# Batch 0 of an attention and mixer kernel: the first weights are decoded earlier, the last tile's products with v stand ahead of the turning, and the two blocks alternate from chunk 0

## The chip, the core and the metric

The kernel runs on one core of a Trainium2 chip. The metric is the device time of one execution in microseconds (us), and the time of a kernel is the median of its runs. TensorE (PE in the profile) multiplies, VectorE (DVE) and ScalarE (ACT) work on vectors, GpSimd (POOL) does a few copies, and SyncE (SP) issues the transfers between memory and the chip's buffers (DMA). Each engine takes its instructions strictly in the order in which they were written into its queue; semaphores hold an instruction back until its data or its buffer is there.

## What is computed

The reference, cut to what matters (four batches of 768 tokens, 8 heads of 64; the mixer's weights are 64-bit floats):

```python
# attention: chunks of 32 queries; each sees 16 keys to the left, its own 32, 8 to the right, and 8 memory slots
scores = scale * np.matmul(q_c, k_full.transpose(0, 1, 3, 2))
a = softmax(scores)                      # row maximum taken off, sum + 1e-9
out[:, :, c_start:c_end] = np.matmul(a, v_full)
# mixer, on x = attention's output, (4, 768, 512)
h = x.transpose(0, 2, 1) @ U @ V         # U 768x32, V 32x768
u = x + h.transpose(0, 2, 1)
ch = np.maximum(u @ w_ch1, 0.0) @ w_ch2  # 512 -> 2048 -> 512
return u + ch
```

## The kernel before

**Tiles and blocks.** A batch's 768 tokens are six tiles of 128 for the mixer (`xs[(b, t)]`), and two blocks of three tiles. Attention works in three tiles T of 256 tokens: `k_part` and `q_part` turn k and q, `s_turn` multiplies them, `s_weights` and `s_sums` make the softmax, `t_part` turns the weights, and `av_part(T)` (line 618) multiplies them with v and lets VectorE scale the product into two tiles x (line 629). `collect(t)` (line 641) sums x times U over all six tiles in one bank; the sum `g` is split into a high and a low part (lines 894 and 895).

**The mixer's input, transposed.** The mixer needs u transposed, a chunk c of 128 channels at a time, four chunks. For batch 0, `turn_x` (line 934) turns block 0 of x by multiplying it with the identity, and leaves the banks open; `join_uT` (line 943) adds V times g to the same banks, and ScalarE and VectorE split each sum into `uh` and `ul` (lines 947 and 948). `turn_x1` and `join_uT1` (lines 958, 975, 979 and 980) do the same for block 1, a chunk at a time.

**Weights.** w1 and w2 come as 64-bit floats in 16 chunks f of 128 hidden channels. The generator `stream` decodes them. A decode is: ScalarE takes the high word of each number (`begin`, line 202); VectorE shifts (209), masks (217), multiplies the low word in (222) and adds (229); ScalarE casts the sum to the high part (340); VectorE subtracts to get the low part (344). The pieces of chunks 0 and 1 (w1 and w2 of each apart) have 512 numbers a row, later ones 1024. `advance(n)` runs `stream` up to its n-th next `yield`: where `advance` stands in the program is where the decode's instructions stand in the queues of ScalarE and VectorE.

**The feed-forward part.** A step of a block with a chunk f is `w1_step` (line 1205: 12 products, high by high, low by high, high by low, into one bank; then ScalarE makes `hh`, line 1213, and VectorE `hl`, line 1214) and, one step later, `w2_step` (lines 1256 and 1262: 9 products into three accumulators). `both_blocks` runs the steps of batch 0. Its list `units` takes block 0 and block 1 in turn for chunks 0 to 10 (`SPLIT` is 11), block 1 `LEAD` chunks behind block 0, and then chunks 11 to 15 of one block after the other. Block 1's accumulators are the three banks of `ps_a` up to unit 21; VectorE adds them to x in unit 22 (line 1221), and the turning of batch 1's keys (line 486), which starts in unit 23, takes the same banks.

**What sets the order.** TensorE's and SyncE's queues stand as the program is written. VectorE's does up to unit 22 and ScalarE's up to unit 2; from there a scheduler orders them by priorities, and the steps' `hh` and `hl` have a high one. `keep_clock(n)` puts n products of a tile of zeros ahead of the next bank's use (line 131).

Of the kernel before, what the change touches and what calls it, by code (L numbers as in the profile page):

```python
# [30 lines left out]
CHAIN = [2, 4]  # L31
WLO = 4
HIGH = 400
LEAD = 1
SPLIT = 11
EARLY = 5
NDEC = 3
# [17 lines left out]
def chunk_attn_then_mixer_kernel(  # L55
# [79 lines left out]
    def keep_clock(n):  # L135

        warm[0] += n
# [213 lines left out]
    def stream():  # L351

        work = [[(f, n)] for f in range(NSOLO) for n in range(2)] + [[(f, 0), (f, 1)] for f in range(NSOLO, NF)]

        def ready(n):
            return n < len(work) and work[n][0][0] in staged and not (front[0] and len(work[n]) > 1)

        def begun(n):
            words = Words([raw for f, which in work[n] for raw in staged[f][which]], nc.vector)
            words.begin()  # L360
            return words

        while not ready(0):
            yield
        ahead, before = begun(0), []
        yield
        for n, parts in enumerate(work):
            while ahead is None and not ready(n):
                yield
            words, ahead = ahead or begun(n), None  # L370
            words.shift()
            if before:
                if len(parts) > 1:
                    yield
                for part in before:
                    lower(*part)
            if ready(n + 1):
                ahead = begun(n + 1)
            yield
            words.power()  # L380
            if len(parts) > 1:
                yield
            words.mantissa()
            yield
            val = words.join()
            before = [(f, which, val[:, 512 * m:512 * m + 512]) for m, (f, which) in enumerate(parts)]
            before = [part + upper(*part) for part in before]
            yield
        for part in before:
            lower(*part)  # L390
        yield
# [13 lines left out]
    def attention(b, xs):  # L405
# [246 lines left out]
        if b == 0:  # L652
# [89 lines left out]
            for t in two:  # L742
                collect(t)
            yield
            av_part(1)
            spread_v(val)
            advance(1)
            for t in two:
                collect(2 + t)
            wide[0] = None  # L750
            early = turn_x()
            advance(3)
            yield
            keep_clock(GAP[3])
            av_part(2)
            advance(1)
            keep_clock(CHAIN[0])
            for t in range(4, NT):
                collect(t)
            turned.extend(turn_x1(c) for c in range(2))  # L760
            yield
        else:
            mv = sm.tile([P, 4 * D], F32, name="mv")
# [133 lines left out]
            )  # L897
        if b == 0:
            join_uT(early, g3)
            for c in range(2):  # L900
                join_uT1(turned[c], c, g3)
            rest.extend((c, g3) for c in range(2, NCK))
        yield "joined"
        if b > 1:
            yield
# [19 lines left out]
    uT = {}  # L925
    w1ls = {}

    def turn_x():

        banks = [ps_h.tile([P, 512], F32, name="ps_h") for _ in range(2)]  # L930
        banks += [ps_o.tile([P, 512], F32, name=f"acc{i}") for i in range(2)]
        for c in range(NCK):
            for tt in range(TB):
                nc.tensor.matmul(
                    out=banks[c][:, tt * P:(tt + 1) * P], lhsT=xs[(0, tt)][:, c * P:(c + 1) * P],
                    rhs=ident, start=(tt == 0), stop=False, skip_group_check=True,
                )
        return banks
# [257 lines left out]

    def w1_step(b, blk, f, w1l, between=lambda: None):
        uh, ul = uT[(b, blk)]
        ph = att_ps() if f == 0 and (b, blk) == (0, 0) else ps_h.tile([P, 512], F32, name="ps_h")
        parts = [(w1h[f], uh, c) for c in range(NCK)] + [(w1l, uh, c) for c in range(NCK)]  # L1200
        parts += [(w1h[f], ul, c) for c in range(NCK)]
        if f > 1 or (b, blk) != (0, 0):
            parts = [part for c in range(NCK) for part in (parts[c], parts[8 + c])] + parts[4:8]
        for m, (w, u, c) in enumerate(parts):
            nc.tensor.matmul(  # L1205
                out=ph[:, :TOK], lhsT=w[:, c, :], rhs=u[c], start=(m == 0), stop=(m + 1 == len(parts)),
            )
            if m + 1 == len(parts) // 2:
                between()
        hh = hid.tile([P, TOK], F32R, name="hh")  # L1210
        hl = hid.tile([P, TOK], F32R, name="hl")
        with tc.high_priority(offset=HIGH):
            nc.scalar.activation(out=hh, in_=ph[:, :TOK], func=AF.Relu)  # L1213
            nc.vector.scalar_tensor_tensor(  # L1214
                out=hl, in0=ph[:, :TOK], scalar=0.0, in1=hh.bitcast(F32), op0=ALU.max, op1=ALU.subtract,
            )
        return hh, hl
# [53 lines left out]
    def both_blocks(following):  # L1271
# [12 lines left out]
        for n, (blk, f, where, begins, ends) in enumerate(units):  # L1284
# [20 lines left out]
                    next(gen[0])  # L1305
                    taken[0] += 1

            hid_ = w1_step(0, blk, f, w1l, between)
            if n == 1:
                for c, g3 in rest:  # L1310
                    join_uT1(turn_x1(c), c, g3)
            for _ in range(RATE + (n % 4 > 0)):
                advance(1)
                more_w()
# [134 lines left out]
```

## Time and profile before

| | us |
|---|---|
| median of 3 runs | 683.27 (681.65 to 685.68) |
| the profiled execution's own time | 685.91 |
| its span, first to last instruction | 683.8 |
| TensorE busy | 648.7 |
| VectorE busy | 345.2 |
| ScalarE busy | 234.7 |
| DMA, mean over the span | 156 GB/s |

The span is what the instructions fill; the execution's own time has 2.1 us around it. A busy TensorE may still run at half its clock: the profile gives the granted clock beside the busy time. A wait is listed as "engine, what it writes, its line <- engine, what it wrote, its line", with the total, the number and the longest.

### The profile page before, as it was taken

Reading aid. Unit: us, or ns where it says so; the run is one execution under the profiler, and the core shown is the slowest. Engines: PE = TensorE matmul, PEld = TensorE weight load, DVE = VectorE, ACT = ScalarE, POOL = GpSimd, SP = SyncE. Lnnn points to the kernel's source line nnn. Section 1 sums busy time; section 2 is a strip of 40 time slices with the busy share of each in tenths; the row PEclk is TensorE's granted clock in tenths of the full one; section 3 lists DMA queues with packets and bytes.
Section 4 is the critical chain, followed back from the end, with each engine's and each line's share of the span. In section 5 each row is a group of like instructions: output and inputs, shape, how many; then the busy total and the mean of one; then the engine's idle time right before and its main releaser. Section 6 shows DMA issues by size and latency. Waiting matters only on the chain.

```text
span 683.8 us, 15135 instructions
## 1 busy us (share of the span) xinstructions
PE 648.7 (95%) x6184; PEld 563.7 (82%) x6188; DVE 345.2 (50%) x681; ACT 234.7 (34%) x574; POOL 63.0 (9%) x95
## 2 busy tenths in 40 slices
PE   7776999998999899999999998999999999999997
PEld 4555999997877599898888887999978889999886
DVE  5847777799554443426424562434436732222322
ACT  4524434434622125323122433434223611212221
POOL 2000000021100042233343000000000000000000
PEclk9998999999999999999999999999999999999999
DMA  8887265434571296762955449884733035555301
GB/s 234 156 254 273 94 210 168 154 118 135 132 149 49 84 271 183 217 205 86 288 191 157 139 129 253 203 207 130 195 104 108 1 108 166 172 144 180 123 2 46
DMA packets 121548, 106.37 MB, mean 156 GB/s; under 512 B 51240, under 2 KB 91048, under 8 KB 121480
## 3 DMA queue, kind: packets, MB, share of 16 engines
q1 hardware_dynamic: 121480, 105.41, 53.1%
q8 instruction: 49, 0.80, 0.5%
q14 instruction: 19, 0.16, 0.1%
HBM read 79.30 MB, written 25.17 MB: 153 GB/s over the span
## 4 chain that ended last, share of the span: by engine, by line
PE 86%; DVE 5%; SPq 3%; DMA 2%; issue 2%; ACT 1%; ACTq 0%; DVEq 0%
PE acc L1256 22%; PE ps_h L1205 19%; PE ps_h L1134 18%; PE acc L1262 11%; PE ps_a L618 2%; PE ps_a L486 2%; PE ps_a L545 2%; PE ps_a L1256 2%; PE ps_a L599 1%; PE acc L641 1%; PE acc L1250 1%; PE ps_a L908 1%; DMA w1l<-w1s 1%; PE ps_a L647 1%; PE ps_a L1262 1%
## 5 line engine op out<-in xcount | busy, mean ns | idle before, releaser
L1256 PE MATMUL acc<-w,hh 128*128 128x512 f32 x606 | 159.5, 398 | 0.0
L1256 PEld LDWEIGHTS acc<-w,hh 128*128 128x128 f32 x606 | 111.1, 189 | 21.3 <-issue 1.0
L1205 PE MATMUL ps_h<-uh,w1h 128*128 128x384 f32 x252 | 87.4, 349 | 7.3 <-ACT w1h L340 6.6
L1262 PE MATMUL acc<-w,hl 128*128 128x512 f32 x303 | 87.6, 397 | 0.0
L1205 PE MATMUL ps_h<-ul,w1h 128*128 128x384 f32 x252 | 85.8, 343 | 1.8 <-DVE ul L997 1.8
L1214 DVE SCALAR_TENSOR_TENSOR hl<-ps_h,hh 128x384 fp32r<-128x384 f32 x63 | 35.0, 555 | 88.5 <-ACT hh L1213 88.4
L1213 ACT ACTIVATE hh<-ps_h 128x384 fp32r<-128x384 f32 x63 | 30.8, 489 | 125.3 <-PE ps_h L1205 125.3
L1262 PEld LDWEIGHTS acc<-w,hl 128*128 128x128 f32 x303 | 55.5, 188 | 11.8 <-issue 0.8
L1205 PEld LDWEIGHTS ps_h<-uh,w1h 128*128 128x128 f32 x252 | 48.3, 192 | 10.5 <-ACT w1h L340 6.9
L1205 PE MATMUL ps_h<-uh,w1l 128*128 128x384 f32 x252 | 56.4, 347 | 0.0
L1205 PEld LDWEIGHTS ps_h<-ul,w1h 128*128 128x128 f32 x252 | 48.5, 192 | 4.4 <-DVE ul L997 2.1
L1205 PEld LDWEIGHTS ps_h<-uh,w1l 128*128 128x128 f32 x252 | 46.4, 193 | 0.0
L1134 PE MATMUL ps_h<-t34h,w1l 128*128 128x384 f32 x128 | 39.4, 349 | 0.0
L1134 PE MATMUL ps_h<-bh,w1l 128*128 128x384 f32 x128 | 36.7, 346 | 2.5 <-DMA w1l<-w1s 2.5
L1134 PE MATMUL ps_h<-t12h,w1l 128*128 128x384 f32 x128 | 37.4, 347 | 0.0
L1151 DVE TENSOR_TENSOR c<-ps_h,c 128x384 f32<-128x384 f32 x16 | 8.9, 558 | 55.3 <-PE ps_h L1134 54.6
L1144 DVE SCALAR_TENSOR_TENSOR hl<-hst,hh 128x384 fp32r<-128x384 f32 x32 | 17.8, 556 | 27.8 <-PE acc L1262 27.7
L1151 DVE TENSOR_TENSOR hst<-ps_h,hst 128x384 f32<-128x384 f32 x32 | 17.8, 555 | 24.2 <-ACT hst L1155 24.2
L1143 ACT ACTIVATE hh<-hst 128x384 fp32r<-128x384 f32 x32 | 16.8, 525 | 36.8 <-PE acc L1256 32.4
L1020 POOL TENSOR_TENSOR vb<-w1h,w1l 128x512 f32<-128x512 f32 x16 | 20.6, 1294 | 92.0 <-DMA w1l<-w1ld 92.0
L910 DVE TENSOR_TENSOR x<-ps_a,x 128x512 f32<-128x512 f32 x24 | 16.4, 689 | 23.1 <-PE ps_a L908 23.1
L1134 PEld LDWEIGHTS ps_h<-bh,w1l 128*128 128x128 f32 x128 | 24.0, 192 | 3.4 <-issue 2.8
(233 smaller groups left out, 1088.5 us busy)
## 6 DMA issues: line engine op xcount, KB each, us to landing
w1l<-w1s SPq DMA_DIRECT2D x112, 256.0 KB
w1l<-w1ld SPq DMA_DIRECT2D x35, 256.0 KB
w1s<-sums SPq DMA_DIRECT2D x32, 256.0 KB
rw<-in_moe_w_ch_dram SPq DMA_DIRECT2D x14, 512.0 KB
qraw<-in_q_dram SPq DMA_DIRECT2D x24, 256.0 KB
out_dram<-x SPq DMA_DIRECT2D x24, 256.0 KB
vb<-in_v_dram SPq DMA_DIRECT2D x56, 98.0 KB
raw<-in_moe_w_ch_dram SPq DMA_DIRECT2D x20, 256.0 KB
```

The source lines that it names most:

```text
L486: nc.tensor.transpose(out=psv[:, p, r, :], in_=half[:, r, 2 * p:2 * p + 2, :].rearrange("n h d -> n (h d)"), identity=ident,)
L910: nc.vector.tensor_tensor(out=x, in0=hp, in1=x, op=ALU.add)
L1020: nc.gpsimd.tensor_tensor(out=v2 if odd else v1, in0=hi, in1=lo, op=ALU.add)
L1134: nc.tensor.matmul(out=ps[:, :TOK], lhsT=w_, rhs=u, start=(start and m == 0), stop=(m == 5), skip_group_check=True,)
L1143: nc.scalar.activation(out=hh, in_=c, func=AF.Relu)
L1144: nc.vector.scalar_tensor_tensor(out=hl, in0=c, scalar=0.0, in1=hh.bitcast(F32), op0=ALU.max, op1=ALU.subtract,)
L1151: nc.vector.tensor_tensor(out=out, in0=ps[:, :TOK], in1=in1, op=ALU.add)
L1205: nc.tensor.matmul(out=ph[:, :TOK], lhsT=w[:, c, :], rhs=u[c], start=(m == 0), stop=(m + 1 == len(parts)),)
L1213: nc.scalar.activation(out=hh, in_=ph[:, :TOK], func=AF.Relu)
L1214: nc.vector.scalar_tensor_tensor(out=hl, in0=ph[:, :TOK], scalar=0.0, in1=hh.bitcast(F32), op0=ALU.max, op1=ALU.subtract,)
L1256: nc.tensor.matmul(out=acc[tt], lhsT=h[:, sl], rhs=w, start=(begins and m == 0), stop=False,)
L1262: nc.tensor.matmul(out=acc[tt], lhsT=hl[:, sl], rhs=w2h[f], start=False, stop=ends is not None)
```

## The change

Line numbers of the kernel before are used for both kernels in the text; in the changed kernel the same statements stand 2 to 6 lines further down.

- **Decode.** `advance(5)` now stands ahead of `av_part(1)`, `advance(3)` behind the sums of tiles 2 and 3, `advance(2)` behind `av_part(2)`, and another ahead of the joins. `stream` yields at the same points for short and long pieces, and begins a short piece's successor after `mantissa` and not after `shift`.
- **Order on TensorE.** `turn_x` is split by chunks: `av_part(2)` stands ahead of all of it, chunks 0 and 1 are turned behind `av_part(2)`, then come the sums of tiles 4 and 5, then chunks 2 and 3.
- **Block 1's chunks.** Three of block 1's four chunks (two before) are turned and joined ahead of the first step; the fourth is turned inside the first step, between its sixth and seventh product (before, chunks 2 and 3 behind the second step).
- **The units.** `LEAD` is 0: the first steps are (block 0, chunk 0), (block 1, chunk 0), (0, 1), (1, 1) and so on, where they were (0, 0), (0, 1), (1, 0), (0, 2), (1, 1). The first step takes the bank `acc2`, and not one of `ps_a`.

```diff
-LEAD = 1
+LEAD = 0
...
             if before:
-                if len(parts) > 1:
-                    yield
+                yield
                 for part in before:
                     lower(*part)
-            if ready(n + 1):
+            if len(parts) > 1 and ready(n + 1):
                 ahead = begun(n + 1)
             yield
             words.power()
-            if len(parts) > 1:
-                yield
+            yield
             words.mantissa()
             yield
+            if ahead is None and ready(n + 1):
+                ahead = begun(n + 1)
...
             yield
+            advance(5)
             av_part(1)
             spread_v(val)
-            advance(1)
             for t in two:
                 collect(2 + t)
+            advance(3)
             wide[0] = None
-            early = turn_x()
-            advance(3)
             yield
             keep_clock(GAP[3])
             av_part(2)
-            advance(1)
-            keep_clock(CHAIN[0])
+            advance(2)
+            early = turn_x(two)
             for t in range(4, NT):
                 collect(t)
-            turned.extend(turn_x1(c) for c in range(2))
+            early += turn_x(range(2, NCK))
+            keep_clock(CHAIN[0])
+            turned.extend(turn_x1(c) for c in range(3))
+            advance(2)
             yield
...
             join_uT(early, g3)
-            for c in range(2):
+            for c in range(3):
                 join_uT1(turned[c], c, g3)
-            rest.extend((c, g3) for c in range(2, NCK))
+            rest.extend((c, g3) for c in range(3, NCK))
...
-    def turn_x():
+    def turn_x(cs):
-        banks = [ps_h.tile([P, 512], F32, name="ps_h") for _ in range(2)]
-        banks += [ps_o.tile([P, 512], F32, name=f"acc{i}") for i in range(2)]
-        for c in range(NCK):
+        banks = []
+        for c in cs:
+            ps = ps_h.tile([P, 512], F32, name="ps_h") if c < 2 else ps_o.tile([P, 512], F32, name=f"acc{c - 2}")
+            banks.append(ps)
             for tt in range(TB):
                 nc.tensor.matmul(
-                    out=banks[c][:, tt * P:(tt + 1) * P], lhsT=xs[(0, tt)][:, c * P:(c + 1) * P],
+                    out=ps[:, tt * P:(tt + 1) * P], lhsT=xs[(0, tt)][:, c * P:(c + 1) * P],
...
-        ph = att_ps() if f == 0 and (b, blk) == (0, 0) else ps_h.tile([P, 512], F32, name="ps_h")
+        first_step = f == 0 and (b, blk) == (0, 0)
+        ph = ps_o.tile([P, 512], F32, name="acc2") if first_step else ps_h.tile([P, 512], F32, name="ps_h")
...
-            hid_ = w1_step(0, blk, f, w1l, between)
-            if n == 1:
+            def joins():
                 for c, g3 in rest:
                     join_uT1(turn_x1(c), c, g3)
+                advance(2)
+
+            hid_ = w1_step(0, blk, f, w1l, between if n else joins)
```

What this makes of the queues is shown at two places. First, VectorE around attention's tiles 1 and 2 of batch 0; `x<-ps_a,rs` is the scaling behind `av_part` (line 629), `dec` the buffer of a decode, `rw_213` and `raw` the raw words of w1's chunk 0, and line 581 ends the softmax sums of tile 2. One piece of the difference:

```order
 L580 TENSOR_SCALAR rs<-rs 128x16
 L581 RECIPROCAL rs<-rs 128x16
+L209 TENSOR_SCALAR dec<-dec 128x512
+L217 TENSOR_SCALAR dec<-dec 128x512
+L222 SCALAR_TENSOR_TENSOR dec<-rw_213,dec 128x256
+L222 SCALAR_TENSOR_TENSOR dec<-raw,dec 128x256
+L229 TENSOR_TENSOR dec<-dec 128x512
 L629 TENSOR_TENSOR x<-ps_a,rs 128x256
 L629 TENSOR_TENSOR x<-ps_h,rs 128x256
```

Five instructions, the decode of w1's chunk 0, moved from behind tile 1's x to ahead of it. Further down in VectorE's queue, before (`rw_217` is w2's chunk 0, `g_983` the sum with U, `ul` block 0's low part, `ul_1003` block 1's):

```order
L229 TENSOR_TENSOR dec<-dec 128x512
L629 TENSOR_TENSOR x<-ps_a,rs 128x256 x4
L209 TENSOR_SCALAR dec<-dec 128x512
L344 TENSOR_TENSOR w1l<-dec,w1h_889 128x512
L895 TENSOR_TENSOR g_983<-acc_341,g_983 32x256 x2
L948 TENSOR_TENSOR ul<-ps_h,uh 128x384 x2
L948 TENSOR_TENSOR ul<-acc_868,uh 128x384
L948 TENSOR_TENSOR ul<-acc_869,uh 128x384
L980 TENSOR_TENSOR ul_1003<-ps_a,uh_1002 128x384 x2
L217 TENSOR_SCALAR dec<-dec 128x512
L222 SCALAR_TENSOR_TENSOR dec<-rw_217,dec 128x512
L229 TENSOR_TENSOR dec<-dec 128x512
```

and in the changed kernel (the last row is the low part of w2's chunk 0):

```order
L209 TENSOR_SCALAR dec<-dec 128x512
L344 TENSOR_TENSOR w1l<-dec,w1h_787 128x512
L217 TENSOR_SCALAR dec<-dec 128x512
L629 TENSOR_TENSOR x<-ps_a,rs 128x256 x4
L222 SCALAR_TENSOR_TENSOR dec<-rw_217,dec 128x512
L229 TENSOR_TENSOR dec<-dec 128x512
L209 TENSOR_SCALAR dec<-dec 128x512
L344 TENSOR_TENSOR w_958<-dec,w_958 128x512
```

The decode of w2's chunk 0 stood behind the six splits of `uh` and `ul`; now it ends ahead of the sum `g`.

Second, VectorE at the end of the alternating units, where block 1's accumulators are added to x (`x<-ps_a,x`, three of them). `hl` is unit 22's, `vb_108` and `vb_109` hold decodes of 1024 numbers a row. Before:

```order
L229 TENSOR_TENSOR vb_108<-vb_108 128x1024
L1214 SCALAR_TENSOR_TENSOR hl<-ps_h,hh 128x384
L229 TENSOR_TENSOR vb_109<-vb_109 128x1024
L1221 TENSOR_TENSOR x<-ps_a,x 128x512 x3
L344 TENSOR_TENSOR w1l<-vb_108,w1h_1913 128x512
```

and in the changed kernel:

```order
L222 SCALAR_TENSOR_TENSOR vb_108<-rw_1617,vb_108 128x512
L209 TENSOR_SCALAR vb_109<-vb_109 128x1024
L1218 SCALAR_TENSOR_TENSOR hl<-ps_h,hh 128x384
L1225 TENSOR_TENSOR x<-ps_a,x 128x512 x3
L229 TENSOR_TENSOR vb_108<-vb_108 128x1024
```

Both joins (line 229) that stood ahead of the three additions stand behind them now.

## The prediction

> **What bounds the kernel now.** The page gives TensorE 648.7 of 683.8 us, so time is won only where it waits or runs slowly. I read first the list of TensorE's waits.
>
> ```profile
> PE ps_h L1205 <- ACT w1h L340: 6.6, 1, 6.6
> PE ps_a L486 <- DVE x L1221: 3.0, 1, 3.0
> PE ps_h L618 <- issue: 2.8, 1, 2.8
> ```
>
> The longest is the second step's wait for the high part of w1's chunk 1. Second, the chain of waits around it (start, length, what):
>
> ```profile
> 42.90 1.89 PE ps_h L934 x12
> 44.78 1.34 PE acc L934 x12
> ...
> 46.55 1.48 PE ps_a L618 x91
> 48.03 0.75 DVE x L629 x2
> ...
> 48.82 1.96 PE acc L641 x4
> ...
> 51.05 1.50 PE ps_a L958 x12
> 52.55 0.19 PE ps_h L943
> ...
> 53.34 1.88 DVE ul L948 x4
> ...
> 62.21 0.63 ACT w1h L340
> ...
> 62.88 4.21 PE ps_h L1205 x12
> ...
> 69.19 1.38 PE acc L1256 x6
> 70.57 0.69 PE acc L1262 x3
> 71.25 2.10 PE ps_h L1205 x12
> ```
>
> TensorE stops at 56.3 (62.88 less the wait of 6.6) and then needs 4.21 us for twelve products that take 2.10 at 71.25. Third, the stretches of 3.41 us by granted clock (columns: stretch, its length, busy time of PE, PEld, DVE, ACT, POOL, clock, DMA share, GB/s):
>
> ```profile
> 37.10:40.51 3.41, 1.63 (x18) 0.69 (x18) 1.47 (x5) 0.92 (x4) 0.00 (x0) 1.00 0.72 153
> 40.51:43.92 3.41, 3.41 (x9) 2.04 (x9) 3.28 (x8) 1.20 (x3) 0.00 (x0) 0.50 0.64 183
> 54.16:57.58 3.42, 2.12 (x10) 1.60 (x10) 3.35 (x8) 0.99 (x3) 0.00 (x0) 1.00 1.06 400
> 57.58:60.99 3.41, 0.00 (x0) 0.00 (x0) 2.71 (x7) 1.57 (x3) 0.00 (x0) 1.00 0.78 297
> 60.99:67.82 6.83, 4.94 (x17) 4.95 (x18) 5.28 (x11) 4.08 (x9) 0.00 (x0) 0.50 0.46 145
> 163.39:166.80 3.41, 3.41 (x13) 3.02 (x13) 3.41 (x7) 2.50 (x10) 0.00 (x0) 0.50 0.39 122
> ```
>
> A stretch with 1.63 us of work is followed by one at half clock, one with 2.12 is not. So the wait costs twice: 6.6 us, and half of the 4.94 us of work at half clock behind it, 2.47. The second wait of the list,
>
> ```profile
> 162.57 0.30 PE L486 MATMUL ps_a<-ident,kn 128*128 128x128 f32 x1 [3.04 <-DVE x L1221]
> ```
>
> costs 3.04 plus half of the 3.41 at half clock behind it: 4.75.
>
> Why is chunk 1 late? VectorE's timeline (the bracket is the idle time before):
>
> ```profile
> 39.01 0.42 DVE L629 TENSOR_TENSOR x<-ps_a,rs 128x256 f32<-128x256 f32 x1 [3.91 <-PE ps_h L618]
> ...
> 41.57 0.43 DVE L209 TENSOR_SCALAR dec<-dec 128x512 int32<-128x512 int32 x1
> ...
> 43.29 0.69 DVE L229 TENSOR_TENSOR dec<-dec 128x512 f32<-128x512 f32 x1
> 48.01 1.42 DVE L629 TENSOR_TENSOR x<-ps_a,rs 128x256 f32<-128x256 f32 x4 [4.03 <-PE ps_a L618]
> ```
>
> It idles 3.91 us and 4.03 us behind the softmax sums and behind its first decode, each time for a tile's products with v, and decodes the rest when the joins are over.
>
> **The change, part by part.** I follow TensorE from 42.90, up to which its queue is the same, to the end of the first step's `w2_step`. Before, that is at 71.25, with two `w1_step`s and all eight joins done; in the changed kernel the same work is done at the same mark, so the difference of the two times is the gain.
>
> *Decode ahead of tile 1's x.* Five instructions now stand ahead of 39.01. They took 2.41 us (41.57 to 43.98). VectorE is free from 35.10 (39.01 less 3.91), ScalarE's copies take 0.43 more, and the words must have landed:
>
> ```profile
> 30.14 0.46 SPq L300 DMA_DIRECT2D raw<-in_moe_w_ch_dram  x1
> ```
> ```profile
> 31.10:36.00 4.90, 4.75 (x126) 2.57 (x125) 3.83 (x11) 0.59 (x1) 0.00 (x0) 0.74 1.11 257
> ```
> ```profile
> 40.72 0.43 ACT L202 ACTIVATE dec<-raw 128x256 f32<-128x256 f32 x1
> ```
>
> The two halves are issued by 30.60 and are read, without a wait, from 40.72. Between 31.10 and 36.00 the DMA moved 4.90 x 257 KB = 1.26 MB, more than chunk 0's 1 MB. I take 36.0 as the landing: 36.0 + 0.43 + 2.41 = 38.84, just ahead of 39.01, cost nothing. The bounds: nothing, and, landing only at 40.72, 40.72 + 0.43 + 2.41 - 39.01 = 4.55 us, since x and all behind it queue behind the decode.
>
> *Products with v ahead of the turning.* From 42.90: two warming products at half clock 0.85 (they took 46.12 to 46.55 at full), products with v 1.48: 45.23. VectorE makes tile 4's x in 0.75 (row 48.03), hidden behind six turnings of 1.34: 46.57. The sums 1.96: 48.53; six more turnings 1.34: 49.87; warming 0.27 (50.78 to 51.05): 50.14; nine turnings of block 1 at 1.50 for six, 2.25: 52.39. Meanwhile `g` is split: before, that took at most from 50.78 to the first join at 52.55, 1.77; now 48.53 + 1.77 = 50.30, plus up to 0.69 behind the low part of w2's chunk 0, which stands ahead of it on VectorE: hidden with 1.4 to spare. The wait of 0.79 for x (48.03 to 48.82) and the one for `g` are gone.
>
> *Joins and first step.* Seven joins of 0.19 from 52.39: 53.72. The first four products need all four `uh`; the fourth `uh` was there before the fourth `ul` began, three quarters of 1.88 after 53.34, so at most 2.2 after the first join: 54.6; three products of 0.175 (2.10 / 12): 55.1. Now the fourth chunk's turning needs a bank that VectorE frees: `ul` of block 0 ran from 0.79 after the first join (53.34 against 52.55) for 1.88, then one more of 0.5: 52.39 + 0.79 + 1.88 + 0.5 = 55.56. TensorE waits 0.4 to 0.7, a new wait inside the step; behind it on TensorE stand six products of the step, and ScalarE's `hh` waits for those. The stretch keeps more than 2.12 us of work, so the clock stays. Turning 0.67 (half of 1.34) and join 0.19: 56.4; six products: 57.5; the second step's twelve 2.10: 59.6; `w2_step` 1.38 + 0.69: **61.6**. The gain at the mark is 71.25 - 61.6 = 9.65 us.
>
> *Chunk 1 in the changed kernel.* VectorE ends block 1's last `ul` some 1.2 after its join at 56.4 (0.79 + 0.5 as above): 57.6. Mask and two low words at 0.43 (41.57 to 43.29 is four such), `hl` 0.55, join 0.69: 60.1; ScalarE's cast 0.63: 60.8, ahead of 61.6. A second `hl` waits for its `hh`, which stands behind the cast: 61.3 + 0.55 + the low part's 0.69 = 62.5, due after four products, at 62.3: a wait of 0.2. Then w2's chunk 1 (0.43 + 0.69 + 0.69), a shift (0.68), a low part (0.69) and `hl` (0.55): 66.2; chunk 2's mask, low words and join (0.68 + 1.7 + 1.21) and its cast: 70.4, due at 61.8 + 2 x 4.15 = 70.1: a wait of 0.3. I take 0.5 for both; the bounds are 0 and 1.5 (VectorE's 12 us a tenth slower).
>
> After that the decode gains on TensorE:
>
> ```profile
> 79.60:120.00 40.40, 40.40 (x206) 37.01 (x205) 31.29 (x51) 17.16 (x37) 0.00 (x0) 1.00 0.53 175
> ```
>
> VectorE works 31.29 of 40.40 us here, 6.43 of the 8.30 us of a pair of steps (2 x 4.15). With `LEAD` 0 a chunk is due one step later than before in the list, and the rate is the same. The number of products, transfers and decodes doesn't change; In SyncE's queue one store of w1's low part (line 322), which waits for VectorE, now stands ahead of chunk 3's loads; chunk 3 is due in the seventh step, and the store's data is made before tile 2's x.
>
> *Unit 22.* In VectorE's queue two joins of 1024 numbers leave the place ahead of the additions that free `ps_a`:
>
> ```profile
> 153.07 0.55 DVE L1214 SCALAR_TENSOR_TENSOR hl<-ps_h,hh 128x384 fp32r<-128x384 f32 x1
> ```
> ```profile
> 160.14 0.54 DVE L1214 SCALAR_TENSOR_TENSOR hl<-ps_h,hh 128x384 fp32r<-128x384 f32 x1
> 160.61 1.21 DVE L229 TENSOR_TENSOR vb<-vb 128x1024 f32<-128x1024 f32 x1
> 161.74 0.68 DVE L1221 TENSOR_TENSOR x<-ps_a,x 128x512 f32<-128x512 f32 x1
> ```
> ```profile
> L222 DVE SCALAR_TENSOR_TENSOR vb<-rw,vb 128x512 f32<-128x512 uint32 (+1 forms) x11 | 6.2, 565 | 0.1
> ...
> L344 DVE TENSOR_TENSOR w1l<-vb,w1h 128x512 fp32r<-128x512 f32 x5 | 3.4, 686 | 0.2
> L217 DVE TENSOR_SCALAR vb<-vb 128x1024 int32<-128x1024 int32 x5 | 3.4, 685 | 0.0
> ```
>
> From unit 21's `hl` to the first addition it took 8.67 us. Now there stand between them one join (1.21), three shifts and masks (0.685 each), two low parts (0.686 each), a chunk's low words (three, at most 1.7) and two `hl` (0.55 each): 7.4 us at the means of 79.6 to 120 (last fence), and 8.7 if the list without `hl` runs a fifth slower beside GpSimd's copies. The wait of 3.04 shrinks by 1.3 or not at all; I take 1.0, so 2.0 is left, and half a chance of the half clock (0.85): 2.85 in place of 4.75, a gain of 1.9. Bounds: 0, and 3.0 (1.7 left, clock kept).
>
> [...]
>
> [...]
>
> **The sum.** -9.65 + 0.5 - 1.9 = -11.05. The profiled execution of 685.91 (span 683.8) would become 674.9. It lies 2.64 above the median of the runs, so against the median: 683.27 - 11.05 = **672.2**.
>
> **The rivals.**
> *Late words.* w1's chunk 0 lands near 40.7; VectorE, strictly in order, holds tile 1's x behind the decode. For: 1.11 as DMA share, the queues are full. Against: the bytes. Price 4.55: 676.7.
> *The decode stays the bound.* Chunks 1 to 3 each come late, since VectorE has done less of its list at the mark. Waits 1.5 instead of 0.5, and unit 22 gains nothing: 683.27 - 8.15 = 675.1.
> *Given back.* Batch 1's keys are loaded by the list of pieces, and GpSimd waited for them:
>
> ```profile
> 148.20 1.58 POOL L435 COPY kn<-kraw 128x512 f32<-128x512 f32 x2 [121.92 <-DMA kraw<-in_k_dram]
> ```
>
> If their landing doesn't come earlier with TensorE, unit 23 waits out the gain of the front: some 682.5. Against: these copies end 12.8 us before the turning that needs them (162.57), and SyncE issues the loads where the pieces stand.
> *Slower.* In the alternating units VectorE needs more than 8.30 us a pair, from 1.29 times its 6.43 on. If its low parts ran as the next row has them, 1.09 against 0.69, a pair would take 10.2, and ten pairs 19 us more: 683.27 - 9.2 + 19 = 693.
>
> ```profile
> 150.24 1.09 DVE L344 TENSOR_TENSOR w1l<-vb,w1h 128x512 fp32r<-128x512 f32 x1
> ```
>
> Against: those long ones came beside GpSimd's copies, and GpSimd did nothing for 121.92 us before 148.20.
>
> **How the numbers follow.** Forecast 0.72, late words 0.10, decode bound 0.09, given back or nothing done 0.05, slower 0.04. A measurement of this kernel tells 0.5%, 3.4 us, from no change. Faster by more: the first three, 0.91, less 0.02 for a mishap with code loading (the 2.8 us wait that names no releaser, which may come again at a new place): 0.89. Within: 0.06. Slower: 0.05. The range: the most that can come off is 9.65 + 3.0 = 12.65, 670.6, and half the spread of the runs shown (681.65 to 685.68) is 2.0: 668.6; late words, 676.7, with the same 2.0 make the upper end, 678.7.
>
> **What would show it.** Right: no wait of 6.6 for `w1h`; VectorE's two idle stretches filled or gone; `w2_step` of the first step ending near 61.6; no half clock between 44 and 150; a wait of less than 3 at line 486. Wrong: x of tile 1 later than 39.0, waits for `w1h` or `w1l` in many units, or TensorE waiting for keys in unit 23.

## The result, and the profile after

| | before | changed |
|---|---|---|
| median of 15 runs, us | 681.85 | 676.03 |
| ratio, 95% interval | | 0.9909 (0.9886 to 0.9931) |
| the profiled execution's own time, us | 685.91 | 673.55 |
| its span, us | 683.8 | 671.6 |
| TensorE busy, us | 648.7 | 642.6 |

The change is faster by 6.2 us (681.85 x 0.0091; by the interval 4.7 to 7.8). The forecast was 11.05. One run of the changed kernel, 1712.74 us, was disturbed and is left out of the ratio.

The list of TensorE's waits, changed kernel (line numbers are now those of its own text: as before up to line 641, 2 to 6 higher from line 889 on; "issue" means that the trace shows nothing that ended the wait):

```profile
PE ps_a L618 <- issue: 2.9, 3, 1.1
...
PE ps_a L486 <- DVE pt L568: 1.9, 1, 1.9
PE ps_h L618 <- issue: 1.9, 1, 1.9
...
PE ps_a L486 <- DVE x L1225: 1.5, 1, 1.5
```

The 6.6 for `w1h` is gone, and the 3.0 in front of batch 1's keys is now 1.5. New is a wait of 1.9 at the same line 486, for `pt`, a softmax of batch 1. The chain of waits from the second group of sums with U to the end of the first step's `w2_step` (start, length, what):

```profile
41.46 2.08 PE acc L641 x3
43.54 0.22 PE ps_a L131
43.90 1.28 PE ps_a L618 x77
45.19 0.79 issue
45.98 0.42 PE ps_a L618 x23
46.40 1.53 PE ps_h L937 x12
47.93 1.72 PE acc L641 x4
49.65 1.34 PE acc L937 x12
...
51.26 2.17 PE ps_a L961 x18
53.43 0.19 PE ps_h L946
...
60.94 1.36 PE acc L1260 x6
62.30 0.69 PE acc L1266 x3
62.99 1.08 PE ps_h L1209 x6
```

The sums end at 43.54 and the mark, the end of the first `w2_step`, is at 62.99, so 19.45 us; before it was 42.90 to 71.25, 28.35. Inside the moved products with v TensorE stands for 0.79, and the trace names nothing that ended this wait.

VectorE and ScalarE at the moved decode (timelines; the bracket is the idle time before):

```profile
36.62 0.46 ACT L202 ACTIVATE dec<-raw 128x256 f32<-128x256 f32 x1 [0.32 <-DMA raw<-in_moe_w_ch_dram]
```
```profile
37.11 0.43 DVE L209 TENSOR_SCALAR dec<-dec 128x512 int32<-128x512 int32 x1 [1.30 <-ACT dec L202]
...
38.83 0.69 DVE L229 TENSOR_TENSOR dec<-dec 128x512 f32<-128x512 f32 x1
39.44 0.42 DVE L629 TENSOR_TENSOR x<-ps_a,rs 128x256 f32<-128x256 f32 x1
```

The words of chunk 0 were waited for until 36.62; tile 1's x then follows the decode with no idle time, at 39.44. It lost nothing by that here: the last of tile 1's products with v ended at 39.39.

The new wait, on TensorE and then on VectorE:

```profile
173.55 0.63 PE L486 MATMUL ps_a<-ident,kn 128*128 128x128 f32 x4 [1.93 <-DVE pt L568]
```
```profile
170.76 0.55 DVE L1218 SCALAR_TENSOR_TENSOR hl<-ps_h,hh 128x384 fp32r<-128x384 f32 x1
171.38 0.18 DVE L555 MEMSET ps_a<- 32x64 f32 x2
171.52 1.29 DVE L567 TENSOR_REDUCE mx<-ps_a 128x8 f32<-128x512 f32 x2
172.73 1.27 DVE L568 TENSOR_TENSOR pt<-ps_a,mx 128x512 f32<-128x512 f32 x2
```

A turning of batch 1's keys needs a bank of `ps_a`, and the two banks of scores are read by VectorE until 174.0. In the kernel before, VectorE had time to spare at the same place, 2.75 us ahead of the addition that comes before this `hl`:

```profile
178.99 0.69 DVE L910 TENSOR_TENSOR x<-ps_a,x 128x512 f32<-128x512 f32 x1 [2.75 <-PE ps_a L908]
```

In the changed kernel the same addition (line 912, 169.18) has no idle time before it. This `hl` starts 9 us earlier than before (170.76 against 179.60), the last low part of the decode ends only 5 earlier (170.84 against 176.24).

### The profile page after: what moved, and what is told of

It reads as the page before. It is cut to its first block, busy times and chain, and to the rows that moved or that the text cites. A ratio compares the mean times of both kernels' runs of the same rounds, so it can differ in the third digit from the quotient of the medians.

```text
span 671.6 us, 15133 instructions
## 1 busy us (share of the span) xinstructions
PE 642.6 (96%) x6184; PEld 557.3 (83%) x6188; DVE 343.9 (51%) x681; ACT 234.2 (35%) x574; POOL 64.1 (10%) x95
## 2 busy tenths in 40 slices
DMA packets 121548, 106.37 MB, mean 158 GB/s; under 512 B 51240, under 2 KB 91048, under 8 KB 121480
## 3 DMA queue, kind: packets, MB, share of 16 engines
q1 hardware_dynamic: 121480, 105.41, 54.2%
## 4 chain that ended last, share of the span: by engine, by line
PE 85%; DVE 8%; DMA 3%; issue 2%; ACT 1%; SPq 1%; POOL 0%; ACTq 0%; DVEq 0%; POOLq 0%
PE acc L1260 22%; PE ps_h L1209 18%; PE ps_h L1137 17%; PE acc L1266 11%; PE ps_a L618 3%; PE ps_a L545 2%; PE ps_a L1260 2%; PE ps_a L486 2%; DMA w1l<-w1s 1%; PE acc L641 1%; PE ps_a L599 1%; DMA kraw<-in_k_dram 1%; PE acc L1254 1%; PE ps_a L1266 1%; DVE x L1225 1%
## 5 line engine op out<-in xcount | busy, mean ns | idle before, releaser
L1158 ACT COPY c<-ps_h 128x384 f32<-128x384 f32 x16 | 7.7, 480 | 52.6 <-PE ps_h L1137 52.6
```

## The experiments

Each kernel has 8 to 15 timed runs ("both of these" and the last three rows 6), against 11 to 35 of the kernel before on the same chip. The columns are the ratio of times, the end of the second sums, the mark, and the stretch between the two, from one profile each. "Second sums" are the products with U of tiles 2 and 3.

| kernel | ratio (95%) | second sums end | mark | stretch |
|---|---|---|---|---|
| before | | 42.90 | 71.25 | 28.35 |
| before, again | 0.9981 (0.9954 to 1.0009) | 40.54 | 68.66 | 28.12 |
| changed | 0.9909 (0.9886 to 0.9931) | 43.54 | 62.99 | 19.45 |
| changed, again | 0.9931 (0.9900 to 0.9962) | 43.99 | 62.72 | 18.73 |
| decode alone | 0.9986 (0.9960 to 1.0012) | 45.49 | 70.12 | 24.63 |
| order alone | 1.0034 (1.0008 to 1.0060) | 40.08 | 72.27 | 32.19 |
| order and `LEAD` 0 | 0.9991 (0.9970 to 1.0012) | 44.25 | 65.13 | 20.88 |
| decode behind x | 0.9925 (0.9898 to 0.9952) | 41.48 | 63.77 | 22.29 |
| turnings around `av_part(2)` | 0.9917 (0.9883 to 0.9950) | 42.91 | 61.35 | 18.44 |
| both of these | 0.9873 (0.9836 to 0.9911) | 41.36 | 60.14 | 18.78 |
| table, one place | 0.9876 (0.9849 to 0.9904) | 43.38 | 63.00 | 19.62 |
| table, both places | 0.9831 (0.9803 to 0.9859) | 43.93 | 62.66 | 18.73 |
| turnings and table | 0.9844 (0.9812 to 0.9877) | 44.06 | 62.52 | 18.46 |
| all three | 0.9847 (0.9820 to 0.9874) | 43.28 | 62.18 | 18.90 |

### The kernel before, again

> The kernel before, unchanged: how its own executions differ. Theory (the profiled execution of before was a bad one): the profiled execution of 683.8 us ran at a mean clock of 0.981, so 683.8 x 0.019 = 13.0 us were lost to half clock, and the changed kernel's lost 671.6 x 0.008 = 5.4; the stretches of 3.41 us lie at another place against the program in each execution, so a stall falls into one stretch or is cut by two. Then the clock of these runs varies, and their median loss is 8 to 11 us, 2 to 5 below 13.0; the wait of 6.6 for w1's chunk 1 stands in the new profile within 1 us, and the third step starts at 71.25 within 1.5. Rival (the profiled execution is the usual one): median loss 12 to 14, and then the changed kernel must have given back some 5 us in its usual executions. Ratio to before 1.000 within 0.003.

The mean clock of the runs lies between 0.977 and 0.991. Span times one less the clock is called the loss below: the time lost to half clock, and a little more, since it counts idle time in such a stretch too. It is on average 9.6 us in the 35 runs of the kernel before beside this one (median 9.5), and 9.3 in this copy. The execution that the prediction was worked out from lost 13.0, and this copy's profiled one 12.3 (683.3 us at 0.982). So both profiled executions of before were bad ones, as the theory had it. The wait of 6.6 is there again, and the third unit starts at 68.66, not within 1.5 of 71.25: TensorE's wait inside `av_part(1)` was 0.93 here and 2.79 before, and the sums behind it ran at full clock.

### The changed kernel, again

> The changed kernel, unchanged: how its own executions differ. Theory (the profiled execution of it was a good one: no half clock behind the waits at 151.8, 171.6 and 403.9): this profile shows the same waits (1.5 at line 486 for x, 1.9 at line 486 for pt, within 0.2) and a longer span, 673 to 676; the second group of sums with U ends between 41.5 and 45.5, and from there to the end of the first step's w2_step it takes 19 to 20 us again (before: 28.35 and 28.12). Ratio to before 0.989 to 0.993. Rival (the gain of the front is itself a matter of luck): that stretch takes 22 us or more.

673.5 us of span, 18.73 from the sums to the mark, waits of 1.9 and 1.6 at line 486: as the theory had it, the stretch a little shorter than the 19 to 20 it gave. Here the wait of 1.9 costs more than itself. Stretches of 3.41 us by granted clock, of this copy and of the first profile of the changed kernel:

```profile
170.20:173.62 3.42, 1.53 (x10) 1.07 (x9) 3.35 (x8) 1.51 (x6) 0.00 (x0) 1.00 0.54 157
173.62:177.03 3.41, 3.41 (x15) 3.31 (x14) 1.94 (x5) 1.94 (x7) 0.00 (x0) 0.50 0.77 169
```
```profile
169.22:172.63 3.41, 2.40 (x13) 1.65 (x11) 3.34 (x8) 1.61 (x8) 1.07 (x2) 1.00 0.50 144
172.63:176.05 3.42, 2.50 (x18) 2.49 (x19) 3.09 (x7) 2.61 (x8) 0.00 (x0) 1.00 0.65 147
```

In the copy one stretch held the whole wait (1.53 us of work left) and the next ran at half clock, 1.7 us lost; in the first profile two stretches shared it (2.40 and 2.50) and nothing was lost. The loss over all runs of the changed kernel is 6.4 us on average in one series and 6.7 in the other.

### The decode alone

```diff
+            advance(5)
             av_part(1)
             spread_v(val)
-            advance(1)
             for t in two:
                 collect(2 + t)
             wide[0] = None
+            advance(3)
             early = turn_x()
-            advance(3)
             yield
             keep_clock(GAP[3])
             av_part(2)
-            advance(1)
+            advance(2)
...
             turned.extend(turn_x1(c) for c in range(2))
+            advance(2)
```

(and the yields of `stream` as in the change).

> Only the decode is moved (the yields of the stream and the calls of advance); the order on TensorE, LEAD 1 and the two turned chunks are as before. Theory (VectorE's list sets the second step): some 2.9 us of VectorE's work (mask 0.42, low word 0.69, join 0.69, low part 0.69 and 0.4 of cast wait) leave the place between the splits of ul and chunk 1, so the wait of 6.6 for w1h shrinks to about 3.5 and the half clock behind it may go: 3 to 5 us faster, third unit's start near 67. Rival (the order of products and units does it all): the decode is hidden in both places, the wait stays above 6, time as before within 1 us.

The waits of its profile:

```profile
PE ps_h L618 <- issue: 3.7, 1, 3.7
PE ps_h L1206 <- ACT w1h L340: 3.7, 1, 3.7
```

The wait for `w1h` is 3.7, where 3.5 was expected, and the stretch is 3.6 shorter. But the sums end at 45.49, and the time is that of before. So the decode does shorten the list that chunk 1 waits for, but the time didn't follow: right on the wait, wrong on the time. In this profile what is later lies ahead of the second sums, and it isn't the decode: that ended at 39.00, and x waited for TensorE until 41.05, which had stood 3.7 us in `av_part(1)` (first row). Why the other runs gained nothing either stays open.

### The order alone

The split `turn_x` and the new order of `av_part(2)`, turnings and sums; decode calls, `LEAD` and two turned chunks as before.

> Only the order on TensorE is changed (products with v of tiles 4 and 5 ahead of the turning, chunks 0 and 1 turned ahead of the sums, 2 and 3 behind); the decode, LEAD 1 and two turned chunks as before. Theory: the waits for x (0.79) and g (up to 1.5) go, so joins and splits come 1.5 to 2 us earlier, but VectorE's list of decodes behind them is as long as before: the wait for w1h stays at 6 to 7 and only moves 1.5 to 2 earlier: 1 to 2 us faster. Rival (TensorE's own order is what counts): 4 us or more faster, with a shorter wait for w1h.

```profile
PE ps_h L1207 <- ACT w1h L340: 6.6, 1, 6.6
PE ps_a L618 <- issue: 4.7, 3, 2.6
```
```profile
45.22 0.65 PE L618 MATMUL ps_a<-vbe,pt 64*32 64x64 f32 x23 [2.56 <-issue]
```

The wait for `w1h` stays at 6.6, as the theory had it, but the kernel is 0.34% slower. The last row names a cost that this profile shows: 2.56 us in the middle of `av_part(2)`, for nothing that the trace can name, 23 products from its end, and a stretch at half clock behind it.

### The order and `LEAD` 0, without the decode

> The changed kernel without the moved decode: the order on TensorE, three turned chunks, the fourth in the first step and LEAD 0 stay; the stream's yields and the calls of advance are those of before. Theory (the decode placed early is needed too): w2's chunk 0 and the low parts (2.5 us of VectorE) stand behind the splits again, chunk 1's high part comes near 63.3 and its low part later, so the third step waits 1.7 to 3 us: 2 to 4 us slower than the changed kernel, ratio to before 0.994 to 0.997. Rival (LEAD 0 does it all, since the second step needs no new chunk): the time of the changed kernel within 1 us, ratio 0.991, and no wait above 1 us for w1h.

```profile
61.35 0.45 PE L1208 MATMUL ps_h<-uh,w1h 128*128 128x384 f32 x1 [1.14 <-ACT uh L981]
66.88 0.97 PE L1208 MATMUL ps_h<-uh,w1l 128*128 128x384 f32 x4 [0.96 <-DVE w1l L344]
```

Two waits, 2.1 us together, where 1.7 to 3 were expected; the first is for block 1's `uh`, the second for `w1l`, none for `w1h`. The rival falls: `LEAD` 0 doesn't do it all, and the decode is needed. The median is 4.2 us above that of the changed kernel, and the ratio, 0.9991, worse than the 0.994 to 0.997 expected. The two waits are half of it; the average loss to half clock is 2 us higher (8.5 against 6.4).

### The decode of chunk 0 behind tile 1's x

```diff
-            advance(5)
             av_part(1)
             spread_v(val)
+            advance(5)
```

> The changed kernel with one call moved: advance(5), the decode of w1's chunk 0, stands behind tile 1's x and the spreading of v instead of ahead of av_part(1). Theory (the decode holds tile 1's x until 39.5, which costs up to 1.7 us where TensorE gets its products done early; behind x it fits in VectorE's second idle stretch of 3.1 us): 0 to 1.7 us faster than the changed kernel, ratio to before 0.988 to 0.991; the second sums with U start at 38.6 to 40 where no long wait of TensorE without a releaser comes before them, and the third unit still finds chunk 1's words. Rival (the first idle stretch is the free one, the second is needed for the rest of the list): chunk 1 comes late, waits of 1 us or more for w1h, 1 to 3 us slower than the changed kernel.

```profile
45.16 0.63 PE L618 MATMUL ps_a<-vbe,pt 64*32 64x64 f32 x23 [1.92 <-issue]
```

The second sums start at 39.53 and end 2.3 us earlier than in the two profiles of the changed kernel (41.48 against 43.54 and 43.99), and no wait for chunk 1 appears, so the second idle stretch does hold the decode. That the sums are earlier is not shown to come from the edit: x follows the end of tile 1's products by 0.05 us here and in both profiles of the changed kernel, and these products ended earlier (38.67 against 39.39 and 39.50). And 1.92 us are lost inside `av_part(2)`, half clock follows, and the mark is at 63.77. No faster.

### What `av_part` waits for

The page counts 6184 products and 6188 weight loads on TensorE. A queue of its own, called instruction (q8), carries 49 packets, 0.80 MB, so 16 KB each, one for 252 of these instructions. Around the wait of 0.79 in the changed kernel (43.4 to 44.6) the transfers show one of them:

```profile
q8 instruction: 1, 0.02, 5.1%
```

I compared the packets of this queue with TensorE's waits without a releaser inside the three `av_part`s, in all fourteen traces, counting from the start the products, the weight loads and the instructions of TensorE's sequencer. Where such a wait is over 0.15 us, it comes at number 959 in `av_part(0)`, 1471 in `av_part(1)` and 1726 in `av_part(2)`, 256 apart or twice that to within one, in every kernel (2 later in four of them), though in time its beginning moves by up to 3.6 us (35.84 to 39.46 in `av_part(1)`). And the work goes on 1.2 to 1.8 us after a packet's end: from 37.36 to 38.63 and from 35.62 to 37.40 in the two profiles of before, from 44.50 to 45.98 in the changed kernel, from 43.76 to 45.22 with the order alone, from 43.69 to 45.16 with the decode behind x. From the equal counts and these times I take it that TensorE has run out of instructions there. One `av_part` is 128 products of 64 columns with their weight loads, just 256 instructions, in 1.5 us.

### Turnings around `av_part(2)`

```diff
+            early = turn_x(two)
             av_part(2)
             advance(2)
-            early = turn_x(two)
+            early += turn_x(range(2, NCK))
             for t in range(4, NT):
                 collect(t)
-            early += turn_x(range(2, NCK))
```

> The changed kernel with the twelve turnings of block 0 around av_part(2) instead of behind it: chunks 0 and 1 ahead of it, chunks 2 and 3 behind it and ahead of the sums. Theory (TensorE's instructions come from memory in packets of 16 KB, 256 instructions; av_part's small products use up most of a packet in 1.3 us, so two av_parts close together outrun the next packet: 0.79 us in the changed kernel, 2.56 in the kernel with only the order changed; 1.34 us of turnings between them give it time): the wait without a releaser inside av_part(2) is under 0.3, and the stretch from the end of the second sums to the end of the first w2_step is 0.5 to 1 us shorter: 0.5 to 2 us faster than the changed kernel, ratio to before 0.988 to 0.990. Rival (the packet is late because of the queues, wherever the products stand): the wait stays or moves, time as the changed kernel within 0.5 us.

No wait inside `av_part(2)`, and the shortest stretch of all, 18.44. Over all profiles: with turnings between the second sums and `av_part(2)` there is no wait at 1726 (seven profiles, both of before among them); without them it is 0.39, 0.79, 0.94, 1.92, 2.56, and none in two whose sums ended late (43.99 and 43.93; at 44.25 there was still 0.39). So, by the counts above, I take it that the moved products with v outran the next packet. The time is not told apart from the changed kernel's.

### Both edits of the front

> The changed kernel with both edits of the front: the decode of w1's chunk 0 behind tile 1's x, and the twelve turnings of block 0 around av_part(2). Theory (what the earlier x won in the kernel with the decode behind x, 2 us at the end of the second sums, was lost again in a wait of 1.92 inside av_part(2) for the next 16 KB of TensorE's instructions; with turnings in between it has time to arrive): no wait without a releaser above 0.3 inside av_part(2); 18 to 19 us from the end of the second sums to the end of the first w2_step; that step ends at 59 to 61.5 unless the wait inside av_part(1) is over 3 us; 1 to 3 us faster than the changed kernel, ratio to before 0.986 to 0.989. Rival (VectorE's list is what holds the first steps): waits for w1h or for g take the place, ratio as the changed kernel, 0.991 to 0.993.

0.8 us are lost in `av_part(1)` and nothing in `av_part(2)`; `av_part(2)` now runs in one piece behind twelve turnings:

```profile
41.20 1.50 PE L937 MATMUL ps_h<-ident,x 128*128 128x128 f32 x12
43.06 1.48 PE L618 MATMUL ps_a<-vbe,pt 64*32 64x64 f32 x128
```

The mark is at 60.14, 2.7 earlier than in the changed kernel's two profiles, and the ratio is what the theory gave. Its interval still touches that of the changed kernel.

### The table of pieces, one place

`PLACE` says how many pieces of batch 1's attention are done at each of four points of a unit.

```diff
-    25: [13, 14, 15, 16], 26: [17, 18, 20, 22], 27: [23, 24, 25, 26]
+    25: [13, 14, 15, 15], 26: [16, 17, 19, 21], 27: [22, 24, 25, 26]
```

> The changed kernel with four numbers of the table of pieces lowered by one (unit 25: 13, 14, 15, 15; unit 26: 16, 17, 19, 21; unit 27 begins with 22), so that the second turning of batch 1's keys of tile 2 stands one place later, in unit 26's first product list. Theory (the changed kernel gives back 1.9 us in a wait there, and half of a stretch at half clock in those executions where the wait falls into one stretch): no wait at line 486 for pt, 1.9 to 3 us faster than the changed kernel, ratio to before 0.987 to 0.989. Rival (VectorE is simply behind there, and the wait only moves to the next piece or to hl): a wait of 1 us or more a few us later, time as the changed kernel within 0.5 us.

```profile
173.54 0.63 PE L486 MATMUL ps_a<-ident,kn 128*128 128x128 f32 x4 [0.84 <-DVE pt L568]
```

The turning still waits 0.84, since the six products now ahead of it (1.1 us) are less than 1.93; no other wait came. So the wait went only in part. The ratio, 0.9876, is what the theory gave, with a median 2.7 to 3.3 below the two of the changed kernel; the intervals overlap.

### The table of pieces, both places

```diff
-    23: [4, 5, 6, 7], 24: [8, 9, 10, 12], 25: [13, 14, 15, 16],
-    26: [17, 18, 20, 22], 27: [23, 24, 25, 26]
+    23: [3, 5, 6, 7], 24: [8, 9, 10, 12], 25: [13, 14, 15, 15],
+    26: [15, 17, 18, 21], 27: [22, 24, 25, 26]
```

> The changed kernel with the table of pieces alone: unit 23 begins with 3 and has 5 next, unit 25 is 13, 14, 15, 15, unit 26 is 15, 17, 18, 21, unit 27 begins with 22. Theory (the waits of 1.5 and 1.9 at line 486 are there because VectorE frees the banks later than the turnings come, and a turning that comes one or two places later finds the bank free; 0.84 was left with one place): both waits under 0.3, 3 to 4.5 us faster than the changed kernel, ratio to before 0.984 to 0.988. Rival (VectorE has too much to do in units 22 to 27, so the wait goes to the next turning, to line 545 or to hl): a new wait of 1 us or more between 150 and 190, ratio 0.989 or more.

```profile
152.92 0.51 PE L910 MATMUL ps_a<-g,v 96*128 96x512 f32 x1 [0.41 <-DVE x L1225]
153.61 1.23 PE L486 MATMUL ps_a<-ident,kn 128*128 128x128 f32 x8 [0.18 <-DVE x L1225]
...
173.15 0.60 PE L486 MATMUL ps_a<-ident,kn 128*128 128x128 f32 x4
```

Of 1.5 and 1.9 there are 0.6 and 0 left, where under 0.3 was expected for both. Median 671.14 us, ratio 0.9831, a little better than forecast, which is 11.5 us below the kernel before; the interval lies clear of both of the changed kernel's. It is the best version found.

### The table with the edits of the front

> The kernel with the twelve turnings around av_part(2) and the table of pieces as in the kernel with the table alone. Theory: the gains of the two places add up, 0.7 from the front and 3 to 4.5 from units 23 to 26: ratio to before 0.983 to 0.987. Rival (what one place wins is waited out at the next, a transfer or batch 1's landing): not faster than the kernel with the table alone.

> All three edits on the changed kernel: decode of w1's chunk 0 behind tile 1's x, turnings around av_part(2), and the table of pieces. Theory: 1 to 3 us from the front and 3 to 4.5 from units 23 to 26, so 5 to 7 us faster than the changed kernel, ratio to before 0.980 to 0.985. Rival (the front's gain is eaten by the fetch of instructions wherever it is won): ratio as the kernel with the table alone, 0.985 to 0.988.

Both at 0.984 to 0.985, within what was forecast, but no faster than the table alone, so no gain of the front is to be seen on top of it. In these profiles the front was not won: all three kernels with the table have their second sums end at 43.3 to 44.1. In the one with the turnings, TensorE was ready and waited for tile 1's x:

```profile
40.40 2.00 PE L641 MATMUL acc<-x,uarea 128*96 128x512 f32 x2 [1.83 <-DVE x L629]
```
```profile
38.99 0.69 DVE L229 TENSOR_TENSOR dec<-dec 128x512 f32<-128x512 f32 x1
39.60 0.42 DVE L629 TENSOR_TENSOR x<-ps_a,rs 128x256 f32<-128x256 f32 x1
```

There the decode ahead of x does hold x. With all three edits x is free of it, but `av_part(1)` lost 2.5 to a wait without a releaser. Whether the edits of the front pay on top of the table is open.

## Why the prediction was right, and where not

**Right: what bounds the kernel, and the stretch from the sums to the mark.** Predicted 61.6 - 42.90 = 18.7 us; measured 19.45 and 18.73, and the first contains the unforeseen 0.79. Against 28.35 and 28.12 the gain is 8.7 to 9.6, forecast 9.65. The smaller steps hold too: the wait for a bank inside the first step is 0.57 in both profiles (0.4 to 0.7 forecast), and there is no half clock between 44 and 150. Of the two waits charged with 0.5, the one for chunk 2's high part came: its first weight load waits 0.52 for the cast, until 71.43, and the product behind it starts 0.94 after the three `hl` products of line 1266 began (70.49), where it is 0.69 without a wait (62.14 to 62.83). So it cost some 0.25. The parts are worth this only together: neither the decode nor the order alone makes the kernel faster.

**Right: unit 22.** 2.0 were to be left of 3.04, and full clock kept with half a chance; 1.5 and 1.6 were left, and neither profile has half clock behind this wait, while both of before have. At 1.6 it was no longer an even chance: even the stretch that held the whole wait kept 1.84 us of work (149.73 to 153.14 in the copy), and no stretch with that much was followed by half clock (see the clock, below).

**Wrong: "from 42.90, up to which its queue is the same", as a fixed start.** The queue is the same, but the time is not. In the seven profiles with the decode ahead of x the second sums start at 40.64 and end at 43.90 on average; in the seven without it they start at 39.52 and end at 41.98. It looks like the decode's price, but the rows of x say otherwise (the copy of the changed kernel, then the decode alone):

```profile
39.55 0.42 DVE L629 TENSOR_TENSOR x<-ps_a,rs 128x256 f32<-128x256 f32 x1 [0.50 <-PE ps_h L618]
```
```profile
41.05 0.42 DVE L629 TENSOR_TENSOR x<-ps_a,rs 128x256 f32<-128x256 f32 x1 [2.04 <-PE ps_h L618]
```

Here x waits for tile 1's products with v, with the decode done. So the prediction's sign of being wrong, x later than 39.0, did come (39.44 and 39.55 in the changed kernel), but for the products and not for the decode. In six of the seven profiles x starts within 0.06 us of the end of these products, as it does without the decode; in one alone the decode held it, by 1.6 us (row 40.40 above). Of the 1.1 us by which the sums start later, 0.9 is that `av_part(1)` ends later (39.50 against 38.64), half of it its wait for instructions, 2.3 on average against 1.9. The sums themselves take 0.8 longer, since they run partly at half clock in six of these profiles and three of the others: the eight in which `av_part(1)` had stood 1.9 us or more, and the one in which x was held. Whether the decode has a part in the waits for instructions no run shows. The prediction had them only as a mishap of 0.02.

**In part luck: "cost nothing" for the decode ahead of x.** The words were read later than the 36.0 taken, from 36.1 to 37.3, and the decode ended at 39.0 to 40.2, not at 38.84. The 39.01 that the prediction held it against comes from an execution in which `av_part(1)` had stood 2.79 us; in the copy of before, with 0.93, x started at 37.77. Where `av_part(1)` ended at 37.3 to 38.7, as it did in four of the seven profiles without the decode ahead, such a decode would have held x. The bounds, 0 to 4.55, did hold what was measured, 0 in six profiles and 1.6 in one.

**Missing: the wait in unit 25.** The prediction followed VectorE's list to unit 22 and no further, and took "the decode gains on TensorE" from the stretch of 79.6 to 120. It named late keys for unit 23 as the rival, but not a bank. The new wait is 1.9 us, and 1.7 more where half clock follows; the table of pieces took it and most of what was left behind unit 22 away, and won 4.3 to 4.9 us by the medians.

**Mis-sized: the time at full clock.** In the loss as counted above, the sum of -11.05 takes off 4.3 us (half of 6.83 behind the long wait, and half a chance of 1.7) and 6.8 of the rest. In the runs the average loss fell by 3.2 (9.6 to 6.4), and the rest (span less loss) by 2.7, 669.9 to 667.2. So most of the missing 5 us lies in the time at full clock. The wait of 1.9 in unit 25, the 0.79 in one of two profiles, and the sums' later start are what the traces name; how much of each an ordinary run has is not shown, and the rest I didn't find.

That the two pairs of profiles differ by 11.0 us (683.8 and 683.3 against 671.6 and 673.5) is in part luck: taken alone they would have confirmed the forecast. Both profiles of before lie above the medians of their runs (by 2.6 and 5.1), those of the changed kernel at or below (by 0.1 above and 2.5 below). Some 3 us of it is the loss, 13.0 and 12.3 in these two against 9.6 on average; why the rest came out high is open.

**The clock.** The stretches of 3.41 us lay at different places against the program in the two profiles of the changed kernel: at the wait in unit 25 one begins at 169.22 in the first and at 170.20 in the copy (rows above). In fourteen traces a full-speed stretch with up to 1.62 us of work was always followed by half clock, one with 1.84 or more never; in between both occur. In the changed kernel's first profile 1.51 (36.10 to 39.51) was followed by half clock, 1.72 (8.79 to 12.20) was not.

**The rivals.** Late words came in part: they held x in one profile of seven, for 1.6 of the 4.55. The decode did not stay the bound, batch 1's keys were not late, and VectorE kept up through the alternating units. The price of this last rival was worked out wrongly: 10.2 us a pair has all of VectorE's 6.43 stretched as the low parts are, but a pair has only two low parts, so 0.8 more, 7.2 in all, still less than 8.30. The forecast range, 668.6 to 678.7, holds the median.

## What to carry to other kernels

When one place is made faster, walk down the queues of every engine to the end of the part that moves, and ask at each later hand-over of a buffer whether the other engine has the same time to spare as before; here a shift of a few entries in a table of places won 4.3 to 4.9 us where the change itself won 6.2. Average the lost clock over many runs before a stall is priced: one profile shows one position of the stretches of 3.41 us, and both profiles of before lost more to half clock (13.0 and 12.3 us) than the average run (9.6). And before products are moved next to each other, count instructions and not only time: here a block of small products took 256 instructions in 1.5 us, and in five of the seven profiles without turnings ahead of the moved one TensorE stood 0.39 to 2.56 us inside it.

## What was unexpected of the hardware

The page of the changed kernel lists a queue called instruction (q8), 49 packets of 16 KB and 0.5% of the 16 DMA engines' span, beside q1, which moves 105.41 of the 106.37 MB and takes 54.2%; and the waits without a releaser inside the `av_part`s came 256 instructions of TensorE apart, or twice that, to within one. In this kernel's front, with a DMA share of 1.04 and 1.11 (34 to 36 and 36 to 38 in the changed kernel), such a wait was up to 3.9 us (in `av_part(1)`, the order and `LEAD` 0), and the waits differ from execution to execution of one kernel: 2.79 and 0.93 in `av_part(1)` of before, 1.90 and 3.26 in the changed kernel. VectorE's low parts and GpSimd's copies took longer where they met. A copy alone takes 0.6 us (first row, of before), a low part alone 0.69. In the changed kernel:

```profile
172.97 1.18 POOL L435 COPY qn<-qraw 128x512 f32<-128x512 f32 x2
```
```profile
163.11 1.10 DVE L344 TENSOR_TENSOR w1l<-vb,w1h 128x512 fp32r<-128x512 f32 x1
...
168.57 0.69 DVE L344 TENSOR_TENSOR w1l<-vb,w1h 128x512 fp32r<-128x512 f32 x1 [0.74 <-ACT w1h L340]
...
169.78 1.06 DVE L344 TENSOR_TENSOR w2last<-vb,w2last 128x512 fp32r<-128x512 f32 x1
```
```profile
162.72 1.97 POOL L435 COPY kn<-kraw 128x512 f32<-128x512 f32 x2 [11.16 <-DVE hl L1218]
...
168.61 1.68 POOL L435 COPY qn<-qraw 128x512 f32<-128x512 f32 x2
```

The low part at 168.57 started 0.04 us ahead of a copy and kept its 0.69; that copy took 1.12. The three low parts of these rows that started inside a copy (163.11, 164.13 and 169.78) took 1.06 to 1.10, 0.4 us more than 0.69. At 168.6 the low part came first and kept its time, at 169.7 the copy, which took 0.62.
